# A planned attention-and-experts kernel: mask set-up split between engines, the last two query groups projected together, and a new order table

## The chip, the cores and the metric

One NeuronCore of a Trainium2 chip runs the whole program. The metric is the device time of one execution in microseconds (us), as the median of the runs. TensorE (PE) multiplies matrices; VectorE (DVE), ScalarE (ACT) and GpSimd (POOL) do the element-wise work; SyncE (SP) issues most DMA transfers.

## The reference

Two stages. The first is a linear recurrence over 768 positions for 4 batches and 8 heads of 48 channels; its output is laid out as x with 384 channels. The second runs four small experts on x, each a causal softmax attention of width 64 with its own output projection; a gate picks the top two of four and weighs them.

```
# recurrence, for each b, h
cur = outer(u*k_t, v_t);  y_t = r_t @ (state + cur)
state = w_t[:, None] * state + outer(k_t, v_t)
x = y as (B, S, H*D)
# experts
logits = x @ w_gate;  top 2 of 4;  w = softmax over the two
for e in range(4):
    q, k, v = x @ wq[e], x @ wk[e], x @ wv[e]
    a = softmax(causal(q @ k.T / 8))
    out += w[e] * ((a @ v) @ wo[e])     # where e is among the two
```

## The kernel before

**Tiling.** The recurrence runs in nine units (r0 to r8): batch 0 in pieces of 128, 256 and 384 positions, the other batches in two pieces of 384 each. Inside a unit positions go in chunks of 64: two scans along the positions (`suf`, L371, and `pre`, L375, on DVE) give the decay products, `kp` (L379 and L381) scales r and k by them, DMAs of `kp` onto itself rearrange it (L406), and TensorE computes the in-chunk scores (`aps`, L467, masked by `dec_mask` into `am`, L473), the state updates (`ups`, L495), and y as the carried part (`yy`, L538, from the faded states `ys`, L514) plus the in-chunk part (`yy`, L560). y is split into a high and a low part (`xh` L576, `xl` L578), because fp32 products are made here of three fast ones: high*high, low*high, high*low.

**The experts** run in ten groups (m0 to m9) of up to 384 positions. They follow the units, but the last unit is cut in two: m8 has 256 positions of batch 3, m9 the last 128. A group projects x to Q and K for two pairs of experts (`pp`, L658 and L661: 9 matmuls for each of 4 products, moving as many columns as the group has positions), to v and the gate's logits (`vp`, L688), then for each pair and each 128 positions makes scores (`sp`, L757), row maxima (L763, DVE), exponentials (`a`, L769, ACT), transposes (`tp`, L782, copied to `ATa`/`ATb` by L214 on ACT or L216 on DVE), and a*v (`yp`, L814). The gate's small operations stand at L712 to L731, the scaling by 1/sum at L832 to L835, its cut into three bf16 parts at L842 to L846; `gp` (L848) transposes it, `gT` (L850) copies that, `gb` (L860) spreads it with the 0/1 matrix `sel`. `yr` (L865 to L870) multiplies `yp` by it, `yh` (L874) and `yl` (L875) split it, `op` (L888) projects it, and `ob` (L214/L216) goes out by an SP DMA (L893).

**The order.** Nothing is ordered by a scheduler at run time. Each step is announced with `plan.add(kind, {engine: estimate}, function, reads, writes)`, and the table `ORDER` gives, for each place, the step (code // 5) and its engine (code % 5) among those that the step allows. Each engine works its own list in order. Tiles have names with a small number of buffers; a step that needs a buffer still in use waits. PE is kept busy before there is real work, and in gaps of the first units, by filler matmuls on a constant (`warm`): 14 of 512 columns (L931) and as many of 256 columns (L963) as a planned gap holds. These are fixed instructions in the program, 147 of the 256-column kind.

**Masks.** DVE makes all constants: `local` (L254 to L257) the identity and the mask of a chunk, `masks` (L274 to L280) in one block the bf16 identity, the causal mask `cmask`, `onehot`, its sum `pick`, `sel` and `tri`.

Of the kernel before, what the change touches and what calls it, by code (L numbers as in the profile page):

```python
# [10 lines left out]
F32 = mybir.dt.float32  # L11
# [8 lines left out]
C = 64  # L20
# [46 lines left out]
class Slot:  # L67
# [6 lines left out]
    def __call__(self):  # L74
# [17 lines left out]
BOTH = {"DVE": {"dg", "sm", "sa", "suf", "pre", "kt", "mr", "uk", "ur", "ux", "yl", "wsplitqk", "wsplitvg", "wsplito", "gate", "masks", "local"},  # L92
        "POOL": {"sm", "sa", "kt", "mr", "uk", "ur", "dg", "yl", "gate", "g4", "wsplitqk", "wsplitvg", "wsplito"}}
# [102 lines left out]
def rwkv_moe(ctx: ExitStack, tc: tile.TileContext, wkr, nat, uN, uT,  # L196
# [87 lines left out]
    def weights(n, src, cols, parts=1):  # L284
# [28 lines left out]
    def rwkv(k, v0, v1):  # L313
# [118 lines left out]
        def pairs(a, got):  # L432
# [42 lines left out]
            plan.add("am", {"DVE": 2 * t_dve(2 * nt * C)}, masked, aps + ["local"], [(am, b) for b in range(2)])  # L475
# [3 lines left out]
        def chain(nas):  # L479
# [26 lines left out]
            for c in range(nh):  # L506
# [18 lines left out]
        def outputs(got):  # L525
# [23 lines left out]
            for a in (1, 0):  # L549
# [21 lines left out]
                for q in range(2):  # L571
# [3 lines left out]
                    else:  # L575
                        plan.add("xh", {"ACT": t_act(2 * nt * C) + 42}, lambda e, q=q, view=view, summed=summed: nc.scalar.copy(view(0, q), summed(q)),  # L576
# [37 lines left out]
    def moe(k, v0, v1):  # L614
        b, s0, nt = GROUPS[k]
        W = nt * 128
        off = slice(s0 * 128, s0 * 128 + W)
# [12 lines left out]
        BT["s"] = BT["s"] + [s0]  # L630
# [4 lines left out]
        Q = [[sb([128, 384], F32R, f"Q{l}{ep}", f"Q{l}{n0}{ep}") for l in "hl"] for ep in range(2)]  # L635
# [12 lines left out]
        def proj(ep, qk):  # L648
            pp = mbank(f"pp{n0}{ep}{qk}")
            plan.sub = 2 * ep + qk  # L650
            cs = slice(ep * 128, (ep + 1) * 128)
            for k in (1, 0, 2):
                step(0.49 * nt / 3)

                def mm(e, k=k):
                    if plain:
                        w = wqf().rearrange("p (a k c) -> p a k c", a=2, k=3)
                        nc.tensor.matmul(pp()[:, 0:W], w[:, qk, k, cs], xx()[:, k, x0:x0 + W].bitcast(F32), start=k == 1, stop=k == 2)  # L658
# [16 lines left out]

        def vproj(i):
# [17 lines left out]
            plan.add("lg", {"DVE": 70}, lambda e: nc.vector.tensor_copy(lg()[:, i, :], vp()[:, 256:260]), [vp], [(lg, i)])  # L694

        def gates():
# [6 lines left out]

            V = nc.gpsimd
# [12 lines left out]
            def ranks(e):  # L717
                V.tensor_tensor(x_(ge), x_(lg), x_(m1)[:, :, None].to_broadcast([128, nt, E]), op=ALU.subtract)
# [4 lines left out]
            plan.add("gate", {"POOL": 1630}, ranks, lgk + ["masks", m1], [c1, c2, rank, ge])  # L723
# [4 lines left out]
            def norm(e):  # L728
# [464 lines left out]
```

## Time and profile before

| what | value |
|---|---|
| median of 3 runs | 328.79 us (328.03 to 329.52) |
| the profiled execution's own time | 327.85 us |
| its span | 326.1 us |
| PE busy | 316.8 us (97%) |
| DVE busy | 266.0 us (82%) |
| ACT busy | 197.9 us (61%) |
| POOL busy | 133.7 us (41%) |

The span runs from the first instruction to the last; 1.75 us of the execution's time lie around it. "Busy" counts the time in which an engine has an instruction under way; matmul ends are modelled, so a full PE is not PE at its peak. The chain of waits follows the work that ended last back to the start, and tells which engine or transfer each stretch waited for. Timeline rows give start and length in us; a bracket at the end gives how long the engine had been idle and which instruction ended that.

### The profile page before, as it was taken

The page shows a single profiled execution, that of the slowest core. Times are in us where ns is not written, and L with a number is a line of the kernel's source. Part 1 is how long each engine was busy: PE and PEld are TensorE (multiplying, and loading weights), DVE is VectorE, ACT ScalarE, POOL GpSimd, SP SyncE. Part 2 cuts the span into 40 slices and gives each one's busy share as a digit, 9 for nine tenths or more (in the row PEclk, how much of TensorE's full clock was granted, in tenths as well). Part 3 has the DMA queues.
Part 4 walks back from the last instruction along what each step waited for, and adds up shares of the span by engine and source line. Part 5 has one row for each costly group of instructions (what it writes and reads, how often), then busy time and mean ns, then how long its engine had stood idle before and what let it go on. Part 6 is the DMA issues. An engine that isn't in the chain of part 4 may idle for free.

```text
span 326.1 us, 12736 instructions
## 1 busy us (share of the span) xinstructions
PE 316.8 (97%) x5096; PEld 269.9 (83%) x5096; DVE 266.0 (82%) x803; ACT 197.9 (61%) x616; POOL 133.7 (41%) x312
## 2 busy tenths in 40 slices
PE   7999999999999999999999999999999999999985
PEld 3778879889896979879898778998898797987774
DVE  7899979987998799979899997867975774369831
ACT  2057474875898647973486766446646545378752
POOL 5543341565556252432655547434860001331420
PEclk9999999999999999999999999999999999999999
DMA  7954736156434643465655184223410300010021
GB/s 204 322 178 127 251 97 185 42 161 214 161 114 105 193 135 107 152 185 176 187 133 176 38 261 115 62 63 100 112 32 3 86 2 0 11 64 2 1 74 72
DMA packets 17866, 38.36 MB, mean 118 GB/s; under 512 B 3488, under 2 KB 8032, under 8 KB 17808
## 3 DMA queue, kind: packets, MB, share of 16 engines
q1 hardware_dynamic: 17424, 35.79, 36.8%
q0 software_dynamic: 384, 1.78, 1.6%
q8 instruction: 40, 0.66, 0.8%
q14 instruction: 18, 0.15, 0.2%
HBM read 28.14 MB, written 4.72 MB: 101 GB/s over the span
## 4 chain that ended last, share of the span: by engine, by line
PE 88%; DVE 5%; DMA 4%; issue 2%; ACT 0%; SPq 0%; POOL 0%; DVEq 0%; POOLq 0%; ACTq 0%
PE pp L661 16%; PE tp L782 12%; PE yp L814 12%; PE sp L757 11%; PE vp L688 8%; PE op L888 7%; PE yy L560 4%; PE aps L467 4%; PE yy L538 4%; PE ups L495 4%; PE ktp L397 2%; PE warm L963 2%; DMA kp<-kp 2%; DMA out_dram<-ob 1%; DVE a L763 1%
## 5 line engine op out<-in xcount | busy, mean ns | idle before, releaser
L769 ACT ACTIVATE a<-a,mx 128x128 f32<-128x128 f32 (+5 forms) x96 | 63.9, 668 | 23.8 <-DVE mx L763 23.3
L661 PE MATMUL pp<-xx,wh_qk 128*128 128x384 f32 (+2 forms) x216 | 60.6, 331 | 0.0
L782 PE MATMUL tp<-ident,a 128*128 128x128 f32 x336 | 50.0, 278 | 0.4 <-DVE mx L763 0.2
L763 DVE CUSTOM_DVE_ANT_0 a<-sp,cmask 128x384 f32<-128x384 f32 (+4 forms) x96 | 44.4, 495 | 6.7 <-PE sp L757 6.0
L782 PEld LDWEIGHTS tp<-ident,a 128*128 128x128 f32 x336 | 37.5, 141 | 6.3 <-ACT ATa L214 1.6
L661 PEld LDWEIGHTS pp<-xx,wh_qk 128*128 128x128 f32 x216 | 39.0, 189 | 1.1 <-issue 0.6
L814 PE MATMUL yp<-ATa,v_sb 128*64 128x384 f32 (+2 forms) x264 | 35.5, 406 | 0.0
L214 ACT COPY ATa<-tp 128x512 f32<-128x512 f32 (+3 forms) x64 | 29.2, 478 | 8.5 <-PE tp L782 7.6
L661 PE MATMUL pp<-xx,wl_qk 128*128 128x384 f32 (+2 forms) x108 | 34.3, 318 | 0.0
L688 PE MATMUL vp<-wh_vg,xx 128*128 128x260 f32 x138 | 30.8, 290 | 0.0
L814 PEld LDWEIGHTS yp<-ATa,v_sb 128*64 128x64 f32 x264 | 16.8, 136 | 14.1 <-issue 9.1
L371 DVE TENSOR_TENSOR_SCAN suf<-lt,one_suf 128x390 f32<-128x390 f32 (+2 forms) x27 | 24.9, 927 | 0.4 <-DMA lt<-in_wkr_dram 0.4
L375 DVE TENSOR_TENSOR_SCAN pre<-lt,inv_pre 128x390 f32<-128x390 f32 (+2 forms) x27 | 24.1, 893 | 0.3
L688 PEld LDWEIGHTS vp<-wh_vg,xx 128*128 128x128 f32 x138 | 23.5, 188 | 0.1
L757 PE MATMUL sp<-Kh,Qh 64*128 64x384 f32 (+4 forms) x128 | 23.5, 362 | 0.0
L216 DVE COPY ATa<-tp 128x512 f32<-128x512 f32 (+3 forms) x32 | 17.9, 570 | 5.2 <-PE tp L782 5.1
L875 POOL TENSOR_TENSOR yl<-yr,yh 128x384 fp32r<-128x384 f32 (+2 forms) x13 | 11.3, 882 | 25.8 <-ACT yh L874 18.8
L757 PE MATMUL sp<-Kh,Ql 64*128 64x384 f32 (+4 forms) x128 | 20.7, 319 | 0.0
L757 PE MATMUL sp<-Kl,Qh 64*128 64x384 f32 (+4 forms) x128 | 20.7, 319 | 0.0
L963 PE MATMUL warm<-one_suf 128*128 128x256 bf16 x147 | 19.2, 285 | 1.4 <-POOL one_suf L236 1.4
L661 PEld LDWEIGHTS pp<-xx,wl_qk 128*128 128x128 f32 x108 | 20.4, 189 | 0.0
L452 ACT ACTIVATE am<-ident,rk 128x64 f32<-128x64 f32 x76 | 19.8, 350 | 0.0
(387 smaller groups left out, 785.1 us busy)
## 6 DMA issues: line engine op xcount, KB each, us to landing
lt<-in_wkr_dram SPq DMA_DIRECT2D x21, 579.5 KB, 4.5
kr<-in_nat_dram SPq DMA_DIRECT2D x24, 288.0 KB, 3.4
out_dram<-ob SPq DMA_DIRECT2D x24, 192.0 KB, 2.1
nat<-in_nat_dram SPq DMA_DIRECT2D x14, 304.0 KB, 3.1
kp<-kp SPq DMA_DIRECT2D x42, 48.4 KB, 3.3
xx<-xx SPq DMA_DIRECT2D x42, 48.0 KB, 2.4
lt<-in_wkr_dram SPq DMA_DIRECT2D x3, 386.5 KB, 4.3
w_qk<-in_wqk_dram POOLq DMA_DIRECT2D x2, 384.0 KB, 5.9
```

What stands on the lines that cost most here:

```text
L214: nc.scalar.copy(o, i)
L371: plan.add("suf", {"DVE": t_scan(wb)}, lambda e: nc.vector.tensor_tensor_scan(rev(suf(), wb), rev(w_(), wb), rev(one_suf, wb), 0.0, op0=AL ...
L375: plan.add("pre", {"DVE": t_scan(wb)}, lambda e: nc.vector.tensor_tensor_scan(pre()[:, 0:kb], w_()[:, 0:kb], flat(inv_pre[:, 0:nh]), 0.0, ...
L661: nc.tensor.matmul(pp()[:, 0:W], w[:, qk, k, cs], xx()[:, k, x * xw + x0:x * xw + x0 + W], start=(k == 1 and j == 0), stop=(k == j == 2))
L688: nc.tensor.matmul(vp()[:, 0:260], xx()[:, k, x * xw + o.start:x * xw + o.stop], w[:, k, :], start=(k == 1 and j == 0), stop=(k == j == 2))
L757: nc.tensor.matmul(sps[x]()[:, 0:w], q()[p, t], k()[p, o], start=j == 0, stop=j == 2)
L763: plan.add("max", {"DVE": t_dve(w) + T_RED}, lambda e, x=x, a=a, mx=mx, h=h, o=o, m=m, sps=sps: nc.vector.tensor_tensor_reduce(a()[:, o], ...
L769: plan.add("exp", {"ACT": t_exp(n)}, lambda e, x=x, y=y, mx=mx, a=a: nc.scalar.activation(a()[:, 0:n], a()[:, 0:n], AF.Exp, bias=mx[-1](), ...
L782: nc.tensor.transpose(tp()[:, j * 128:(j + 1) * 128], a()[:, (j0 + j) * 128:(j0 + j + 1) * 128], ident)
L814: nc.tensor.matmul(yp()[e * 64:e * 64 + 64, lo:W], v_sb[ep]()[:, j, e * 64:e * 64 + 64], at, start=(j == 0), stop=(j == nj - 1))
L888: nc.tensor.matmul(op()[:, 0:DM], y()[:, t], w[:, ep, :], start=(j + ep == 0), stop=(j == 2 and ep == 1))
L963: nc.tensor.matmul(w()[:, 0:256], wz[:, 0:128], wz[:, 0:256], start=True, stop=True)
```

## The change

1. The set-up steps are cut apart. `local` becomes two steps and `masks` six, each with its own readers; `local`, `cmask`, `tri`, `onehot` and `pick` may run on DVE or POOL, `sel` and the bf16 identity on ACT or DVE. The reduction that made `pick` is two additions.
2. More steps may run on more engines: the high half of a weight (`wsplit`, ACT before) also on DVE and POOL; `ys` (L514) also on ACT, as four small multiplications; `xh`, the high halves of Q and K, `yr` also on DVE; `lg` and `gT` also on ACT; the gate's two small blocks and `g4` also on DVE; `yh` also on DVE and POOL.
3. Group m8 projects 384 columns, its own 256 and the 128 of m9; m9 projects no Q and K, and reads its columns of m8's tiles.
4. `ORDER` is new from its first entry.

```diff
-    def local(e):
-        for t, op in ((ident2, ALU.is_equal), (dec_mask, ALU.is_gt)):
-            nc.vector.tensor_scalar(t[0:64], d128[0:64, 0:C], 0.0, None, op0=op)
-            nc.vector.tensor_scalar(t[64:128], d128[64:128, 0:C], -64.0, None, op0=op)
+    def local(e, t, op):
+        E_[e].tensor_scalar(t[0:64], d128[0:64, 0:C], 0.0, None, op0=op)
+        E_[e].tensor_scalar(t[64:128], d128[64:128, 0:C], -64.0, None, op0=op)
...
-    def masks(e):
-        nc.vector.tensor_copy(identb, ident)
-        nc.vector.tensor_scalar(cmask[:, 384:512], d128, 0.0, -1.0e9, op0=ALU.is_gt, op1=ALU.mult)
-        nc.vector.tensor_scalar(onehot, dcol, drow, None, op0=ALU.is_equal)
-        nc.vector.tensor_reduce(pick, onehot.rearrange("p (a r) -> p r a", a=3), axis=AX.X, op=ALU.add)
-        nc.vector.tensor_copy(sel, pick[:, :, None].to_broadcast([128, 3 * E, HD]))
-        nc.vector.tensor_scalar(tri, tri, 0.0, None, op0=ALU.is_gt)
+    def picked(e):
+        E_[e].tensor_tensor(pick, onehot[:, 0:12], onehot[:, 12:24], op=ALU.add)
+        E_[e].tensor_tensor(pick, pick, onehot[:, 24:36], op=ALU.add)
...
+    masks = [(dict(POOL=350, DVE=200), lambda e: E_[e].tensor_scalar(cmask[:, 384:512], d128, 0.0, -1.0e9, op0=ALU.is_gt, op1=ALU.mult), [], "masks"),
...
+             (dict(ACT=700, DVE=500), lambda e: copy(e, sel, pick[:, :, None].to_broadcast([128, 3 * E, HD])), ["pick"], "sel"),
+             (dict(ACT=170, DVE=150), lambda e: copy(e, identb, ident), [], "identb")]
...
                 def faded(e, y=y, s=s, c=c):
+                    if e == "ACT":
+                        for p in range(NP):
+                            nc.scalar.mul(y[:, p * D:(p + 1) * D], s[0:112, p * D:(p + 1) * D], kp[0:112, p, K0 + c:K0 + c + 1])
+                        return
...
-        BT["s"] = BT["s"] + [s0]
+        tail = k == len(GROUPS) - 1
+        q0, PW = (W0, 0) if tail else (0, 384 if k == len(GROUPS) - 2 else W)
+        if not tail:
+            BT["s"] = BT["s"] + [s0]
...
-                        nc.tensor.matmul(pp()[:, 0:W], w[:, qk, k, cs], xx()[:, k, x * xw + x0:x * xw + x0 + W], start=(k == 1 and j == 0),
+                        nc.tensor.matmul(pp()[:, 0:PW], w[:, qk, k, cs], xx()[:, k, x * xw + x0:x * xw + x0 + PW], start=(k == 1 and j == 0),
...
-            plan.add("gate", {"POOL": 1630}, ranks, lgk + ["masks", m1], [c1, c2, rank, ge])
+            plan.add("gate", {"POOL": 1630, "DVE": 480}, ranks, lgk + ["tri", m1], [c1, c2, rank, ge])
...
-            t = slice(i * 128, (i + 1) * 128)
+            t = slice(q0 + i * 128, q0 + (i + 1) * 128)
...
-            plan.add("g4", {"POOL": 2450}, parts, [gg], [gg, g3])
+            plan.add("g4", {"POOL": 2450, "DVE": 480}, parts, [gg], [gg, g3])
...
-            plan.add("yh", {"ACT": t_act(W) + 42}, lambda e: nc.scalar.copy(h()[:, 0:W], yr()[:, 0:W]), [yr], [h])
+            plan.add("yh", {"ACT": t_act(W) + 42, "DVE": t_dve(W), "POOL": t_pool(W)}, lambda e: copy(e, h()[:, 0:W], yr()[:, 0:W]), [yr], [h])
...
-            for qk in range(2):
+            for qk in range(0 if tail else 2):
...
 ORDER = (
-    234, 448, 1, 159, 6, 154, 161, 175, 183, 202, 205, 166, 171, 17, 22, 27, 32, 37, 42, 47, 52, 57, 62, 67, 72, 77,
+    21, 8, 3, 564, 566, 588, 259, 266, 283, 189, 44, 339, 184, 191, 196, 205, 47, 52, 57, 62, 67, 72, 77, 82, 87, 92,
```

The new table gives the steps to the engines so: of the ten gate blocks of each kind six move from POOL to DVE, of the ten `g4` seven; 7 `xh`, 9 high halves of Q and K, 8 `yr` and 4 `yh` move from ACT to DVE, 8 `yh` from ACT to POOL; 14 `lg`, 4 `gT`, `sel` and the bf16 identity go from DVE to ACT, and 9 `ys` to ACT, 8 of them from DVE; 5 `kp`, 6 `kr` (L424 and L426, r and k scaled by u), 4 `us` (L519), the low half of one weight and both parts of `local` go from DVE to POOL. DVE has 860 instructions where it had 803. There are 149 fillers of 256 columns where there were 147, and 14 of 512 in both. The 36 projections of 256 columns and the 36 of 128 (m8 and m9) are 36 of 384.

**DVE at the start, before**: the block of masks (L256 to L280), then the first scans, those of r0's tiles `lt` (w, k and r of the unit; 130 columns are one of its parts).

```order
L257 TENSOR_SCALAR dec_mask<-d_73 64x64
L275 CAST identb<-ident 128x128
L276 TENSOR_SCALAR cmask<-d_73 128x128
L277 TENSOR_SCALAR onehot<-dcol,drow 128x36
L278 TENSOR_REDUCE pick<-onehot 128x12
L279 CAST sel<-pick 128x768
L280 TENSOR_SCALAR tri<-tri 128x16
L371 SCALAR_TENSOR_TENSOR suf_0_130<-lt_0_121,one_suf 128x130
L373 RECIPROCAL inv_pre<-suf_0_130 128x2
L375 SCALAR_TENSOR_TENSOR pre_0_152<-lt_0_121,inv_pre 128x130
L371 SCALAR_TENSOR_TENSOR suf_0_170<-lt_0_168,one_suf 128x260
```

DVE at the start, now (lines have moved by two: the scans are L373 and L377):

```order
L238 MEMSET inv_pre 128x390
L279 TENSOR_SCALAR onehot<-dcol,drow 128x36
L373 SCALAR_TENSOR_TENSOR suf_0_121<-lt_0_119,one_suf 128x260
L373 SCALAR_TENSOR_TENSOR suf_1_126<-lt_1_124,one_suf 128x130
L373 SCALAR_TENSOR_TENSOR suf_0_135<-lt_0_129,one_suf 128x130
L375 RECIPROCAL inv_pre<-suf_0_135 128x2
L381 TENSOR_TENSOR kp_96<-lt_1_124,suf_1_126 128x128
L377 SCALAR_TENSOR_TENSOR pre_0_153<-lt_0_129,inv_pre 128x130
L274 TENSOR_TENSOR pick<-onehot 128x12
```

One mask step is left ahead of the first scan, and that scan is now one of 260 columns, of unit r1. The constants stand between the scans or on POOL and ACT.

**SP at the start, before**, the loads of `lt` (131 and 256 columns are r0's, 773 r1's, 1159 r2's):

```order
L222 DMA lt_1_114<-in_wkr_dram 128x256
L222 DMA lt_0_121<-in_wkr_dram 128x256
L222 DMA lt_0_121<-in_wkr_dram 128x131
L222 DMA lt_0_168<-in_wkr_dram 128x773
L222 DMA lt_1_114<-in_wkr_dram 128x131
```

SP at the start, now:

```order
L222 DMA lt_0_119<-in_wkr_dram 128x773
L222 DMA lt_1_124<-in_wkr_dram 128x131
L222 DMA lt_0_129<-in_wkr_dram 128x256
L939 DMA u_81<-in_uT_dram 128x56
L222 DMA lt_2_132<-in_wkr_dram 128x256
L222 DMA lt_0_129<-in_wkr_dram 128x131
```

A load of r1 stands ahead of all of r0's.

**DVE at the end, before** (`gg` is the scaling of m9, `ob` an output tile of m7 and then of m8, `gT__6361` m9's gate):

```order
L835 TENSOR_TENSOR gg__6314<-gg__6314,ge__6069 128x4
L870 TENSOR_TENSOR yr_0_6324<-gb_0_6275,yr_0_6324 128x256
L870 TENSOR_TENSOR yr_1_6281<-gb_1_6296,yr_1_6281 128x256
L216 COPY ob_1_6348<-op_1_6307 128x384
L216 COPY ATa_10_6359<-tp_200_6299 128x4x128
L850 COPY gT__6361<-gp__6357 128x128
L216 COPY ob_1_6401<-op_1_6394 128x384
```

DVE at the end, now (the first row is m9's scaling, the five `g__6283` rows its cut into parts):

```order
L847 TENSOR_TENSOR gg__6279<-gg__6279,ge__6124 128x4
L854 MEMSET g__6283 128x64
L855 CAST g__6283<-gg__6279 128x4
L856 TENSOR_TENSOR gg__6279<-gg__6279,g__6283 128x4
L857 CAST g__6283<-gg__6279 128x4
L858 TENSOR_TENSOR g__6283<-gg__6279,g__6283 128x4
L216 COPY ob_0_6289<-op_0_6261 128x384
L887 TENSOR_TENSOR yl_0_6304<-yr_0_6147,yh_0_6302 128x256
L882 TENSOR_TENSOR yr_1_6270<-gb_1_6306,yr_1_6270 128x256
L216 COPY gT__6325<-gp__6323 128x128
```

The cut into parts, which POOL did, stands on DVE. One copy of `ob` stands between it and `gT`, as before, but of m7's first tile; the copies of m7's and m8's other tiles are on ACT.

## Rows read from the trace of the kernel before

**Rows 1.** The page: busy time by engine; the chain's shares by engine

```profile
PE 316.8 (97%) x5096; PEld 269.9 (83%) x5096; DVE 266.0 (82%) x803; ACT 197.9 (61%) x616; POOL 133.7 (41%) x312
...
PE 88%; DVE 5%; DMA 4%; issue 2%; ACT 0%; SPq 0%; POOL 0%; DVEq 0%; POOLq 0%; ACTq 0%
```

**Rows 2.** Windows: length; PE, PEld, DVE, ACT, POOL busy (instructions); clock; DMA

```profile
20.00:30.00 10.00, 9.17 (x173) 7.93 (x171) 10.00 (x20) 6.25 (x22) 4.38 (x7) 1.00 0.40 113
...
160.00:170.00 10.00, 10.00 (x386) 8.94 (x385) 9.62 (x30) 7.34 (x20) 5.00 (x9) 1.00 0.41 112
170.00:180.00 10.00, 10.00 (x78) 8.93 (x79) 10.00 (x31) 7.22 (x22) 5.90 (x11) 1.00 0.60 183
180.00:190.00 10.00, 10.00 (x243) 7.39 (x240) 9.90 (x28) 7.29 (x20) 5.64 (x17) 1.00 0.21 61
310.00:320.00 10.00, 8.83 (x80) 7.84 (x81) 3.15 (x11) 5.03 (x15) 2.19 (x6) 1.00 0.19 66
```

**Rows 3.** Chain of waits, projections of 384, 256 and 128 columns (start, us, matmuls)

```profile
109.04 2.12 PE pp L661 x12
...
260.91 1.75 PE pp L661 x15
...
291.55 0.95 PE pp L661 x9
```

**Rows 4.** Timeline of DVE, the first 6 us

```profile
1.63 0.19 DVE L256 TENSOR_SCALAR ident<-d 64x64 f32<-64x64 f32 x1 [0.36 <-POOL d L242]
...
3.60 0.58 DVE L279 CAST sel<-pick 128x768 bf16<-128x768 f32 x1
...
4.17 0.41 DVE L371 TENSOR_TENSOR_SCAN suf<-lt,one_suf 128x130 f32<-128x130 f32 x1
...
5.79 1.02 DVE L371 TENSOR_TENSOR_SCAN suf<-lt,one_suf 128x260 f32<-128x260 f32 x2 [0.38 <-DMA lt<-in_wkr_dram]
```

**Rows 5.** Chain of waits in the head (SPq: issuing of loads)

```profile
0.74 0.38 SPq L222
...
2.12 3.65 DMA lt<-in_wkr_dram
...
14.37 5.25 DMA kp<-kp
...
22.14 0.82 DVE ys L514
...
23.80 1.31 PE warm L963 x11
```

**Rows 6.** Timeline of PE in the head

```profile
23.01 0.45 PE L538 MATMUL yy<-kp,ys 48*64 48x64 f32 x16 [0.75 <-DVE ys L514]
...
25.19 0.68 PE L560 MATMUL yy<-am,nat 64*64 64x64 f32 x32
```

**Rows 7.** Timeline of DVE, 24 to 30 us: one form twice

```profile
24.94 1.87 DVE L295 TENSOR_TENSOR wl_qk<-w_qk,wh_qk 128x768 fp32r<-128x768 f32 x1
...
28.24 0.92 DVE L295 TENSOR_TENSOR wl_qk<-w_qk,wh_qk 128x768 fp32r<-128x768 f32 x1
```

**Rows 8.** Timeline of POOL beside it

```profile
24.98 1.00 POOL L384 TENSOR_TENSOR lt<-lt 128x384 f32<-128x384 f32 x1
```

**Rows 9.** Timeline of all engines in the tail

```profile
311.11 0.16 DVE L835 TENSOR_TENSOR gg__6314<-gg__6314,ge__6069 128x4 f32<-128x4 f32 x1
...
311.40 0.19 POOL L843 CAST g__6318<-gg__6314 128x4 bf16<-128x4 f32 x1 [2.76 <-DVE gg__6314 L835]
...
315.56 0.56 DVE L216 COPY ob<-op 128x384 f32<-128x384 f32 x1 [2.92 <-DMA out_dram<-ob]
...
316.89 0.22 PE L860 MATMUL gb<-gT__6361,sel 128*128 128x128 bf16 x1 [1.17 <-DVE gT__6361 L850]
```

**Rows 10.** Chain of waits in the tail: a store, and m8's `op`

```profile
311.60 3.83 DMA out_dram<-ob
...
317.34 2.10 PE op L888 x12
```

More of the change, by code (lines that the diff above doesn't have):

```diff
@@ L88 @@
          "SP": dict(PE=1600, DVE=1600, ACT=1600, POOL=1600, SP=1600)}
-BOTH = {"DVE": {"dg", "sm", "sa", "suf", "pre", "kt", "mr", "uk", "ur", "ux", "yl", "wsplitqk", "wsplitvg", "wsplito", "gate", "masks", "local"},
-        "POOL": {"sm", "sa", "kt", "mr", "uk", "ur", "dg", "yl", "gate", "g4", "wsplitqk", "wsplitvg", "wsplito"}}
+BOTH = {"DVE": {"dg", "yh", "g4", "sm", "sa", "suf", "pre", "kt", "mr", "uk", "ur", "ux", "yl", "wsplitqk", "wsplitvg", "wsplito", "gate", "masks", "local"},
+        "POOL": {"masks", "local", "sm", "sa", "kt", "mr", "uk", "ur", "dg", "yl", "gate", "g4", "wsplitqk", "wsplitvg", "wsplito"}}
 class Plan:
@@ L292, in weights @@
             load("wload" + n, lambda o=o: f()[:, o], src[:, o], cols // parts, [(f, c)])
-            plan.add("wsplit" + n, {"ACT": t_act(cols // parts) + 40}, lambda e, o=o: nc.scalar.copy(h[:, o], f()[:, o]),
+            plan.add("wsplit" + n, {"ACT": t_act(cols // parts) + 40, "DVE": t_dve(cols // parts), "POOL": t_pool(cols // parts)}, lambda e, o=o: copy(e, h[:, o], f()[:, o]),
                      [(f, c)], [("wh", n, c)])
@@ L474, in masked @@
                                               aps[h]()[:, 0:2 * nt * C].rearrange("p (a i j) -> p a i j", a=2, j=C))
-            plan.add("am", {"DVE": 2 * t_dve(2 * nt * C)}, masked, aps + ["local"], [(am, b) for b in range(2)])
+            plan.add("am", {"DVE": 2 * t_dve(2 * nt * C)}, masked, aps + ["dec"], [(am, b) for b in range(2)])
         car = [cars[(k + 1) % 2], cars[k % 2]]
@@ L575, in outputs @@
                     else:
-                        plan.add("xh", {"ACT": t_act(2 * nt * C) + 42}, lambda e, q=q, view=view, summed=summed: nc.scalar.copy(view(0, q), summed(q)),
+                        plan.add("xh", {"ACT": t_act(2 * nt * C) + 42, "DVE": t_dve(2 * nt * C)}, lambda e, q=q, view=view, summed=summed: copy(e, view(0, q), summed(q)),
                                  [yy[a][q]], [(xx, a, "h", q)])
@@ L616, in moe @@
         W = nt * 128
-        off = slice(s0 * 128, s0 * 128 + W)
+        W0 = GROUPS[-2][2] * 128
         xx, xk, x0, xw = XS[b, s0]
@@ L634, in rows @@
             return [y for y in xk if y[1] == (k if y[2] == "d" else k % 2)]
-        Q = [[sb([128, 384], F32R, f"Q{l}{ep}", f"Q{l}{n0}{ep}") for l in "hl"] for ep in range(2)]
+        if not tail:
+            BT["Q"] = [[sb([128, 384], F32R, f"Q{l}{ep}", f"Q{l}{n0}{ep}") for l in "hl"] for ep in range(2)]
+        Q = BT["Q"]
         lg = sb([128, 3, E], F32, "lg", f"lg{n0}")
@@ L693, in vproj @@
                          [vp], [(v_sb[ep], s0 + i)])
-            plan.add("lg", {"DVE": 70}, lambda e: nc.vector.tensor_copy(lg()[:, i, :], vp()[:, 256:260]), [vp], [(lg, i)])
+            plan.add("lg", {"DVE": 70, "ACT": 60}, lambda e: copy(e, lg()[:, i, :], vp()[:, 256:260]), [vp], [(lg, i)])
         def gates():
@@ L731, in norm @@
                 V.tensor_scalar(x_(gs), x_(gs), 1e-9, None, op0=ALU.add)
-            plan.add("gate", {"POOL": 875}, norm, [ge, c1], [gs, c1])
+            plan.add("gate", {"POOL": 875, "DVE": 270}, norm, [ge, c1], [gs, c1])
         def scores(ep, i):
-            t = slice(i * 128, (i + 1) * 128)
+            t = slice(q0 + i * 128, q0 + (i + 1) * 128)
             plan.sub = 3 * ep + i
@@ L922, in rwkv_moe @@
     plan.now = -1.0
-    plan.add("local", {"DVE": 1060}, local, [], ["local"])
-    plan.add("masks", {"DVE": 1400}, masks, [], ["masks"])
+    plan.add("local", {"DVE": 530, "POOL": 650}, lambda e: local(e, ident2, ALU.is_equal), [], ["local"])
+    plan.add("local", {"DVE": 530, "POOL": 650}, lambda e: local(e, dec_mask, ALU.is_gt), [], ["dec"])
+    for engs, fn, reads, name in masks:
+        plan.add("masks", engs, fn, reads, [name])
     plan.add("ldu2", {"SP": 475, "ACT": 475}, lambda e: E_[e].dma_start(u2, uT.rearrange("p (j c) -> p j c", j=7)), [], ["u2"], xfer=190.0)
```

37 lines of the change are left out of this document (21 added, 16 removed), and 220 rows, old and new, of the table ORDER.

## Prediction

> **What bounds the kernel now.** I read the busy shares first, then the chain of waits, then windows. TensorE (PE) is busy 97% of the span and carries 88% of the chain; VectorE (DVE) carries 5%, transfers 4%, and the other engines round to nothing [rows 1]. So the time is PE's work plus the places where PE has none. The windows say where these are: PE is full in the middle (10.00 of 10 us in the three windows from 160 us on); it has gaps in the head (9.17 between 20 and 30 us) and in the tail (8.83 between 310 and 320 us) [rows 2]. Three things can therefore shorten the kernel: fewer or cheaper matmuls, an earlier start of the first real work (the fillers hide that the head is a wait: PE counts as busy while it multiplies constants), and a tail with fewer waits. A change of engine for an element-wise step in the middle can win almost nothing, since PE does not wait there; it can only lose, if it makes DVE late. DVE is itself at 9.62, 10.00 and 9.90 of 10 us between 160 and 190 us, and full from 20 to 30 us [rows 2].
>
> **Joint projection, about -1.7 us.** Before, m8 has 36 matmuls of 256 columns and m9 36 of 128; now there are 36 of 384. The pace is read from the chain, which gives stretches of them back to back: 12 of 384 columns take 2.12 us, 177 ns each; 15 of 256 take 1.75 us, 117 ns; 9 of 128 take 0.95 us, 106 ns [rows 3]. The small form is far dearer than its columns: it hardly beats the one of twice the size. The sum: 36 x 117 = 4.21 and 36 x 106 = 3.82, together 8.03; 36 x 177 = 6.37; difference 1.66. All are on PE, and PE is full or nearly so in this stretch, so the whole of it shows. What could take some back: m9's projections were filler between attention steps of m7 and m8, and the exponentials of these may now be waited for; and the joint ones must come before m8's scores. Bounds: 1.3 to 2.1. The evacuations also fall from two per product to one, off PE's path.
>
> **Mask set-up, at most half a microsecond by itself.** The obvious reading is that DVE spends 2.5 us on masks (from 1.63 us to 4.17 us [rows 4]) and that the scans start that much sooner. That is not what the rows say. The next scan in the row, at 5.79 us, waited 0.38 us for a landing, with all masks done [rows 4]; the loads set the pace until then. The scan at 4.17 us started right behind the last mask, so it could have been somewhat sooner, but its data cannot have come much before: the first load was issued by about 1.1 us, and a load of r1, issued at 2.12 us, took 3.65 us to land [rows 5]. I give the masks' removal 0 to 0.5 us. Against it stands the new order of loads: a 386 KB load of r1 is issued ahead of r0's small ones, and the first scan on DVE is r1's. If that scan holds DVE until r1's data land, r0's scans start later than now by up to about 0.6 us (first issued, by 1.12 us, and 3.65 us under way [rows 5], it lands at 4.8 us; r0's scan began at 4.17).
>
> **The rest of the head, -1.5 us with the masks in it.** From the first scan to 14 us DVE is the chain, then the `kp` transfer of 5.25 us, then DVE again, at 22.14 us with `ys` [rows 5]. PE waited 0.75 us for that `ys`, ran y's first half at 23.01 us, 11 fillers, and the second half at 25.19 us [rows 6]. From 20 to 30 us DVE never rests [rows 2], so each microsecond taken from DVE before `ys` brings y, and all behind it, forward by as much. The change takes `sel` (0.58 us [rows 4]), the other constants, and some `ys` and low halves off DVE there, about 2 us of work; `ys` runs partly on ACT, which has room (6.25 of 10 us busy [rows 2]). The ends: +0.5 us if the late load of r0 outweighs it, -2.5 us if all of the relief shows and the 5.25 us transfer also starts sooner. I take -1.5, nearer to the gain, since DVE is the releaser in the row and the masks stand early in its list. The fillers are fixed instructions: 149 instead of 147 at 1.31 / 11 = 0.12 us each [rows 5] cost +0.2 us, and where they stand behind data that come early they go on running.
>
> **Body, 0 with a width of 1.5.** DVE takes over six gate chains, seven `g4` chains, 7 `xh`, 9 halves of Q and K, 8 `yr`, 4 `yh` and gives away less; by the durations of the nearest forms in the trace (0.16 us for a small operation, up to 0.56 us for a copy of 384 columns, both [rows 9]) I estimate some 8 us more for DVE over the whole program, of 60 us that it has free (326.1 - 266.0 [rows 1]). ACT loses some 2 us, POOL is about as before. Work in the free part is hidden; PE's wait would show it where it is not. To win, there is only PE's idle time outside head and tail, about nothing in the windows shown. So the middle is 0, and the ends are -1.5 and +1.5 us.
>
> What the trace says of moving steps to POOL: the same subtraction took 1.87 us on DVE while a POOL instruction of 1.00 us ran, and 0.92 us alone [rows 7, 8]. The difference, 0.95 us, is nearly the POOL instruction's length. The Trainium skill has a rule for this (SBUF — State Buffer, "SBUF: two separate sides"): DVE with two inputs in SBUF and a POOL operation that reads SBUF take an exclusive lock on a shared pair of ports, and the loser waits for the whole instruction. The rows agree. By that rule the 5 `kp`, 6 `kr`, 4 `us` and 8 `yh` given to POOL, 23 steps, would each cost DVE up to a POOL instruction's length again, some 1 us by the row, 23 us in all; it speaks against these moves, and it would change the sum only by the part of them that falls where DVE is full.
>
> **Tail, -0.9 us.** Now, m9's gate is late for a reason that has nothing to do with gates: DVE's copy of `ob` stands ahead of `gT__6361`, and waits 2.92 us for a store (3.83 us in the chain [rows 10]) that still reads the buffer; so `gT` is late, and PE stands 1.17 us before `gb` [rows 9]. In the new order m7's copies are mostly on ACT and the tile ahead of `gT` is its first, so this wait should go. Three things are late next. DVE now cuts m9's scaling itself: 11 small operations at 0.16 to 0.2 us, 2 us, where before three on DVE (from 311.11 us) and five on POOL (the first at 311.40 us, 0.19 us each [rows 9]) took about as long. ACT's copies of `ob` still wait for earlier stores, and behind one of them stands an `ATa` copy that m9's `yp` needs: up to 2.92 us there, of which m8's 12 `op` matmuls on PE hide 2.10 [rows 10]. And the last `yr`, `yh`, `yl` all stand on DVE, which saves the hops to ACT, a few tenths. Following the new rows by hand with these durations I get an end about 1 us sooner, and take -0.9; ends -1.2 (the whole wait of 1.17) and +0.5 us (ACT's wait takes its place and more).
>
> **Sum.** -1.7 - 1.5 + 0.2 + 0 - 0.9 = -3.9 us. Against the profiled execution, 327.85 us, that is 323.95; the median is 328.79, 0.94 above it, and I carry the same difference: 324.9 us.
>
> **Rivals.**
> The head gives nothing (**326.4**, chance 0.20): the first r0 scans wait for loads behind r1's, and fillers stand where data come sooner. Then only -1.7 + 0.2 - 0.9 = -2.4 remains. For it: the wait for a landing at 5.79 us [rows 4] and the fillers that stand in the chain [rows 5]. Against it: DVE's 100% from 20 us on.
> Only the projections, **about 328** (0.15): head as in the rival above, the tail's wait changes its place, fillers +0.2 and a few waits behind projections eat the rest of 1.7. This is within 0.5%, which is about what a measurement of this kernel can tell from no change.
> DVE becomes the bound (**331**, 0.08), the slower side: between 160 and 190 us DVE has 0.48 us free of 30 [rows 2]. If the work it takes over, or meetings with POOL at 0.95 us each, falls there and in the two or three stretches like it, PE waits for row maxima. It decides against the change when such waits exceed the 3.9 us of gains; with 6.1 us of them, six or seven meetings, the time is 328.79 - 3.9 + 6.1 = 331.0. Against it: there are 60 us free elsewhere, and gates and `g4`, whose small POOL operations met DVE's, leave POOL.
> The new order also removes waits that the modelled ends of matmuls hide (**321.5**, 0.15): head at its end of -2.5, body at -1.5, tail at -1.2, joint projections at -2.1, fillers +0.2 give -7.1, that is 321.7, and I set 321.5.
>
> **How the numbers follow.** The forecast itself has 0.42; with 0.20, 0.15, 0.08 and 0.15 that is 1. Faster by over 0.5% means below 327.15: the forecast (0.42), the better order (0.15), most of the head rival (0.15), a little of the projections rival (0.02), 0.74. Slower by over 0.5% means above 330.4: DVE as the bound, 0.07 of its 0.08. The rest, 0.19, is no change. For the range I leave out the slower case, half of the projections rival's upper side and the lower part of the better order, together under 0.2: 320.8 to 328.6.
>
> **What will show it.** Joint projections right: 36 matmuls of 384 columns for m8, none for m9, PE's busy time lower by about 1.7 us, no new idle time of PE beside them. Head right: y's second half (25.19 us now) begins between 22.7 and 25 us, with DVE's `ys` earlier; wrong if it begins at 25.2 us or later, or if the first scans of DVE wait past 5 us. Tail right: no DVE wait of more than a microsecond for a store, and `gb` of m9 without PE idle before it. Body right: PE at 9.9 of 10 us or more in every window from 40 to 300 us; wrong if PE waits there for DVE's maxima or for ACT. The whole is wrong if PE's busy time rises elsewhere, or if DVE near 190 us lags with PE waiting.

## The result: 331.59 us after 329.03, slower by 0.5%

The changed kernel takes 331.59 us (median of 20 runs, 327.79 to 333.45), the kernel before 329.03 us beside it (20 runs, 326.73 to 330.93). The ratio is 1.0052, 95% interval 1.0026 to 1.0077. The forecast was 324.9 us, with a range up to 328.6. The profiled execution took 331.89 us; its span is 330.0 us, 3.9 more than before. Medians are of all runs; the ratios leave out those over 1.5% above the least time of their kernel, so the 0.5% stands for 1.7 us where the medians lie 2.56 us apart.

One remark is needed for every number below: the granted clock of TensorE differs from run to run. The new kernel's five runs at a mean clock of 0.997 or more took 328.0 us, its twelve at 0.990 or less 332.2 us. Of the 136 runs of the kernel before that stand beside the experiments, the 64 at 0.997 or more took 328.2 us, and only six were at 0.990 or less. So at the whole clock the two kernels take the same time, and the new one loses in the runs in which its clock fell.

The page of the new kernel: busy time, the chain's shares, and PE's granted clock in 40 slices (against [rows 1]).

```profile
PE 317.1 (96%) x5062; PEld 269.7 (82%) x5062; DVE 276.4 (84%) x860; ACT 197.9 (60%) x628; POOL 134.8 (41%) x259
...
PE 80%; DVE 9%; issue 3%; ACT 3%; POOL 2%; DMA 1%; SPq 1%; DVEq 0%; POOLq 0%
...
PEclk9999599999999999999999999999999999999999
```

PE's share of the chain fell from 88% to 80%; DVE, ACT and POOL took it. PE's busy time did not fall, although 1.7 us of projections are gone, and one slice runs at half the clock. The windows, with the columns of [rows 2], say where:

```profile
0.00:10.00 10.00, 8.55 (x42) 4.81 (x42) 5.24 (x19) 1.68 (x3) 5.73 (x25) 1.00 0.75 221
...
30.00:40.00 10.00, 8.63 (x129) 8.01 (x130) 5.96 (x13) 4.79 (x19) 4.00 (x5) 0.70 0.37 106
140.00:150.00 10.00, 7.82 (x199) 5.95 (x190) 6.42 (x16) 6.44 (x25) 5.69 (x9) 1.00 0.54 155
...
310.00:320.00 10.00, 10.00 (x96) 8.37 (x95) 8.45 (x35) 4.90 (x13) 0.40 (x1) 1.00 0.01 2
```

DVE is less busy in the first ten microseconds (5.24, before 8.07); PE has gaps and a mean clock of 0.70 from 30 to 40 us, and waits 2.18 us from 140 to 150 us. The tail is full, where [rows 2] had 8.83. The head, in PE's timeline of the new kernel:

```profile
20.35 0.33 PE L497 MATMUL ups<-nat,kts 64*64 64x48 f32 x8 [1.33 <-DVE kts L216]
...
25.27 0.68 PE L566 MATMUL yy<-am,nat 64*64 64x64 f32 x32
...
26.72 3.01 PE L977 MATMUL warm<-one_suf 128*128 128x256 bf16 x26
31.37 0.52 PE L399 MATMUL ktp<-ident,kp 128*128 128x128 f32 x3 [1.64 <-ACT am L454]
```

The second half of r0's y starts where it did (25.27 us against 25.19 [rows 6]). Then 26 fillers run out, and PE stands 1.64 us for r2's first keys (`ktp`). In the kernel before these start 4.2 us sooner:

```profile
27.16 0.53 PE L397 MATMUL ktp<-ident,kp 128*128 128x128 f32 x3
```

From 34 to 41 us the new kernel's clock is at 0.50, one level down (1.2 GHz for 2.4); one window of it (length, PE busy, granted clock, DMA share, GB/s):

```profile
36.00:38.00 2.00, 2.00 (x9) 0.50 0.31 115
```

Around 140 us the new kernel's ACT and PE read:

```profile
141.95 1.54 ACT L454 ACTIVATE am<-ident,rk 128x64 f32<-128x64 f32 x6 [2.88 <-PE yy L566]
...
143.39 0.60 ACT L781 ACTIVATE a<-a,mx 128x384 f32<-128x384 f32 x1
...
144.63 0.44 PE L794 MATMUL tp<-ident,a 128*128 128x128 f32 x2 [2.06 <-ACT a L781]
```

ACT's list has r5's `am` block ahead of two of m3's exponentials. The block needs a buffer that r4's `yy` on PE must free; so ACT idles 2.88 us with the exponentials' data at hand, and PE then waits 2.06 us for them.

### The profile page after: what moved, and what is told of

Its sections match the earlier page's. It is cut to its first block, busy times and chain, and to the rows that moved or that the text cites. A ratio compares the mean times of both kernels' runs of the same rounds, so it can differ in the third digit from the quotient of the medians.

```text
span 330.0 us, 12661 instructions
## 1 busy us (share of the span) xinstructions
PE 317.1 (96%) x5062; PEld 269.7 (82%) x5062; DVE 276.4 (84%) x860; ACT 197.9 (60%) x628; POOL 134.8 (41%) x259
## 4 chain that ended last, share of the span: by engine, by line
PE 80%; DVE 9%; issue 3%; ACT 3%; POOL 2%; DMA 1%; SPq 1%; DVEq 0%; POOLq 0%
PE pp L673 13%; PE tp L794 11%; PE yp L826 11%; PE sp L769 10%; PE op L900 7%; PE vp L700 7%; PE ups L497 4%; PE aps L469 4%; PE yy L544 3%; PE yy L566 3%; PE ktp L399 2%; DVE suf L373 2%; DVE pre L377 2%; ACT am L454 1%; PE rp L392 1%
## 5 line engine op out<-in xcount | busy, mean ns | idle before, releaser
L673 PE MATMUL pp<-xx,wh_qk 128*128 128x384 f32 (+1 forms) x192 | 56.2, 343 | 0.0
L214 ACT COPY ATa<-tp 128x512 f32<-128x512 f32 (+3 forms) x68 | 31.0, 487 | 13.3 <-PE tp L794 12.8
L673 PEld LDWEIGHTS pp<-xx,wh_qk 128*128 128x128 f32 x192 | 34.9, 189 | 0.1
L673 PE MATMUL pp<-xx,wl_qk 128*128 128x384 f32 (+1 forms) x96 | 31.6, 329 | 0.0
L377 DVE TENSOR_TENSOR_SCAN pre<-lt,inv_pre 128x390 f32<-128x390 f32 (+2 forms) x27 | 25.9, 960 | 0.1
L373 DVE TENSOR_TENSOR_SCAN suf<-lt,one_suf 128x390 f32<-128x390 f32 (+2 forms) x27 | 24.1, 902 | 1.4 <-DMA lt<-in_wkr_dram 1.4
L454 ACT ACTIVATE am<-ident,rk 128x64 f32<-128x64 f32 x72 | 18.4, 341 | 7.5 <-PE yy L566 2.9
L216 DVE COPY ATa<-tp 128x512 f32<-128x512 f32 (+3 forms) x28 | 15.1, 544 | 8.8 <-PE tp L794 8.8
L525 POOL TENSOR_TENSOR us<-us,ys 112x192 f32<-112x192 f32 x21 | 12.6, 600 | 19.8 <-DVE pre L377 7.6
L700 PE MATMUL vp<-wl_vg,xx 128*128 128x260 f32 x69 | 19.5, 283 | 0.0
L584 DVE TENSOR_TENSOR xx<-yy,xx 112x384 fp32r<-112x384 f32 (+1 forms) x32 | 16.1, 532 | 4.0 <-ACT xx L214 3.9
```

The costliest lines, as they stand in the source:

```text
L214: nc.scalar.copy(o, i)
L373: plan.add("suf", {"DVE": t_scan(wb)}, lambda e: nc.vector.tensor_tensor_scan(rev(suf(), wb), rev(w_(), wb), rev(one_suf, wb), 0.0, op0=AL ...
L377: plan.add("pre", {"DVE": t_scan(wb)}, lambda e: nc.vector.tensor_tensor_scan(pre()[:, 0:kb], w_()[:, 0:kb], flat(inv_pre[:, 0:nh]), 0.0, ...
L454: nc.scalar.mul(am()[:, h, b, i], ident2, v[:, i, h:h + 1])
L673: nc.tensor.matmul(pp()[:, 0:PW], w[:, qk, k, cs], xx()[:, k, x * xw + x0:x * xw + x0 + PW], start=(k == 1 and j == 0), stop=(k == j == 2))
L700: nc.tensor.matmul(vp()[:, 0:260], xx()[:, k, x * xw + o.start:x * xw + o.stop], w[:, k, :], start=(k == 1 and j == 0), stop=(k == j == 2))
```

## The experiments

Two theories were set against each other. Head: the new order loses in the first 55 us, and the clock with it. Body: it loses by waits of ACT and DVE in the middle. Medians are of 6 to 12 runs; ratios, with 95% intervals, are to the kernel before on the same chip. Where two kernels are compared, the difference of their ratios is taken, times 329 us.

**e1, joint projection alone.**

```diff
 kernel before
+m8 projects 384 columns, m9 none
```

> The kernel before with one change: m8 projects 384 columns and m9 none; the masks on DVE, the engines and the order of all other steps are those of before (the sum of the one-hot rows is two additions). Both theories, head (A: the new order loses in the first 60 us, by late loads of r0, and PE's wait at 30 us is followed by half the clock) and body (B: it loses by waits for ACT and DVE in the middle), expect the forecast of this term: -1.7 us (-1.3 to -2.1), ratio 0.995. If the ratio is 1.000, the term itself was wrong.

Measured: 327.09 us, before 328.87; 0.9946 (0.9909 to 0.9982). The term is right: -1.8 us (by the interval, -3.0 to -0.6).

**e2, head of before.**

```diff
 new kernel
-first 55 us in the new order
+first 55 us in the order and on the engines of before
```

> The new kernel, but every step that the order of before has in its first 55 us stands as it did there, on its engine of before; the rest is in the new order, with the joint projection. A (head): the loss goes, the granted clock stays at 1.00 from 30 to 60 us, and the time is about 326 us, ratio 0.992, 5 us below the new kernel. B (body): the time stays at 329 to 331 us, ratio 1.000 to 1.005.

Measured: 328.26 us, 0.998 (0.9954 to 1.0007); the runs lie between 327.6 and 328.7. The head holds 2.4 us of the new kernel's time. What is left, 1.1 us above e1, is the new order behind 55 us; the intervals of e2 and e1 overlap, and e6 below bears it out. So both theories have a part. The clock did not stay up, as theory A had it: in e2's profiled execution it is at 0.62 and 0.52 from 28 to 32 us, and it falls again right behind PE's wait for ACT, which e2 shares with the new kernel (2.06 us, until 139.76 us); the window has the columns of the one above:

```profile
142.00:146.00 4.00, 4.00 (x64) 0.68 0.45 114
```

**e3, start of before.**

```diff
 new kernel
-first 10 us in the new order
+first 10 us as before (r0's loads first, masks as one block)
```

> The new kernel, but only the first 10 us stand as before: r0's loads first, the masks as one block on DVE; from there on the new order (11 fillers fewer come out of the plan). If the late loads of r0 carry the head's loss: DVE is busy 8 of the first 10 us as before, r2's first keys on PE start 3 us sooner (28 us), the clock stays up, and the time is about 327 us. If the rest of the head's order carries it: r2's keys stay at 30 us or later, 330 us or more.

Measured: 333.04 us, 1.0109 (1.0051 to 1.0167), six runs, five of them at a clock of 0.989 or less. r0's first product on DVE starts at 6.61 us instead of 7.40, and yet r2's keys start at 32.78 us. Undoing the start does not cure the head. But e3 has 11 fillers fewer, which can cost time by itself (e11), so what the late loads alone cost is not shown here.

**e4 and e5, fillers where PE stood idle.**

```diff
 new kernel
+16 fillers ahead of r2's first keys          (e4 and e5)
+14 fillers ahead of r0's state updates       (e5)
```

> The new kernel with 16 more fillers of 256 columns ahead of r2's first keys, where PE stood idle 1.64 us before 31.37 us. If the idle time is what the clock fell for: granted clock 1.00 between 34 and 41 us, time 328.2 us in all runs (the new kernel's runs at clock 1.00 are 327.8 to 328.4). If the clock falls for the few columns of the matmuls after it: clock 0.50 again, 331.6 us.

> The new kernel with 30 more fillers: 14 ahead of r0's state updates, in which PE stood idle 1.33 us before 20.35 us, and 16 ahead of r2's first keys (1.64 us before 31.37 us). With the second place alone the clock was whole in only a few runs (329.8 us). If idle time of PE in the head is what the clock falls for: most runs at granted clock 0.997 or more and the median at 328.0 to 328.6 us. If it falls for other reasons: a spread from 327.4 to 335 us and a median near 330 us, as before.

Measured: e4 329.75 us (1.0007, 0.9966 to 1.0047), in single runs from 327.4 to 335.4; its profiled execution has the clock at half from 22 to 25 us instead, behind the other gap. e5 329.78 us (1.002, 0.9989 to 1.0052), with no run below 0.993 and all between 328.6 and 331.4. So with both gaps filled the deep falls are gone, as the theory of idle time says; but only four of the twelve runs are at 0.997 or more, not most, and the median did not reach 328.0 to 328.6.

**e6 and e9, one step moved on ACT,** in e2 and in the new kernel.

```diff
 ACT, around 142 us
-L454 ACTIVATE am_0_2894<-ident_84,rk_0_2414 128x64 x6
 L781 ACTIVATE a_32_2761,asum__2499<-a_32_2761,mx_320_2762 128x384
 L781 ACTIVATE a_21_2764,asum__2499<-a_21_2764,mx_210_2765 128x256
 L214 COPY yr_0<-yp_0
+L454 ACTIVATE am_0_2894<-ident_84,rk_0_2414 128x64 x6
```

> The kernel e2 (head of before, rest new) with one step moved: on ACT, r5's `am` block (six small steps of 0.25 us, which waits for r4's last use of the buffer on PE) stands behind m3's two exponentials and `yr` instead of ahead of them. PE waited 2.1 us there (136 to 140 us in e2) for the exponentials. If that wait is on the path: 1.5 to 2.1 us less than e2, 326.2 to 326.8 us. If the wait only moves to the next step: 328.2 us as e2.

> The new kernel with the one step of e6 moved (r5's `am` block on ACT behind m3's exponentials), the rest as it is. If the wait there costs the new kernel as it cost e2 (1.8 us): 329.8 us against 331.6. If the clock in the head hides it or the runs spread too far: 331 us.

Measured: e6 326.46 us (0.9922, 0.9891 to 0.9953), 1.9 less than e2, with intervals that do not overlap. e9 328.83 us (1.0006, 0.9975 to 1.0037), 1.5 less than the new kernel (2.8 by the medians of all runs). One step of 1.5 us, three places too early in a list, cost about as much as the joint projection had gained.

**e7, gates back on POOL** (in e2).

```diff
-DVE: 16 gate blocks and cuts into parts, m1 to m9
+POOL: the same, at the same places
```

> The kernel e2 with the gates' small blocks and the cut into parts back on POOL wherever the new order gave them to DVE from m1 on (16 steps; 8 fillers fewer). If DVE's added work and its meetings with POOL make the middle's waits: DVE's busy time falls by 5 to 8 us and the time by 1 to 1.5 us, to about 327 us. If DVE's work there is hidden: 328.2 us or, since POOL takes longer for them, up to 1 us more.

Measured: 329.73 us, 1.003 (1.0001 to 1.0059), 1.6 more than e2. The page of e7, and the longest of PE's waits in it (total us, times, longest):

```profile
PE 314.8 (96%) x5058; PEld 268.7 (82%) x5058; DVE 269.8 (82%) x791; ACT 193.9 (59%) x621; POOL 144.8 (44%) x322
...
PE yy L566 <- POOL nat L553: 2.2, 2, 2.0
```

DVE did get some 8 us less to do (277.7 in e2), and it helped nothing visible. But e7 made a loss of its own: at 190.84 us PE waits 2.00 us for a small POOL step (`nat`) that stands behind a gate's cut into parts, which itself waited for DVE. In e2 this wait is 0.2 us. So e7 does not show that giving DVE the gates was a gain; it shows once more what one step costs that waits ahead of a ready one.

**e8, the new tail alone.**

```diff
 e1
-from 250 us on the order of before
+from 250 us on the new order
```

> The kernel before with the joint projection up to 250 us, and the new order from there. Forecast for the tail: 0.9 us less than e1 (327.1 us), so 326.2 us; the trace of the new kernel gives 1.4 us less idle time of PE between 300 and 320 us, so 325.7 us. If the new tail's waits take the place of the old ones: 327.1 us.

Measured: 329.88 us (1.0023, 0.9989 to 1.0057), 2.5 more than e1. The seam itself made a wait:

```profile
264.77 0.77 PE L794 MATMUL tp<-ident,a 128*128 128x128 f32 x5 [2.61 <-ACT a L781]
```

Without these 2.61 us the time would be about that of e1, if the whole of them is on the path. So the tail gave about nothing, as far as a kernel with a seam can say.

**e10, masks alone,** and **e12, loads alone** (each in e1).

```diff
+e10: masks spread over POOL, ACT and DVE's later list
+e12: SP: r1's 386 KB load ahead of r0's, the first eight loads as in the new kernel
```

> The kernel e1 (before with the joint projection) and the masks of the new kernel: identity and chunk mask on POOL, `sel` and the bf16 identity on ACT, the others between r0's scans on DVE (4 more fillers come out of the plan). By the rows of before (the first scans wait for loads): 0 to -0.5 us against e1, 326.6 to 327.1 us. If the obvious reading held (2.5 us off DVE at the start): 325 us. If it changes nothing but the fillers: 327.5 us.

> The kernel e1 with only the first eight loads on SP in the new order, r1's 386 KB load ahead of r0's (11 more fillers come out of the plan); masks and scans as before. By the prediction: the head starts up to 0.6 us later, 327.1 to 327.7 us. By the new kernel's trace, where r0's first products waited for a landing until 7.4 us: 2 to 3 us later, 329 to 330 us, if r0's scans set the head. 327.1 us if they do not.

Measured: e10 325.94 us (0.9924, 0.9896 to 0.9952, six runs), 0.7 less than e1, with intervals that overlap widely: a gain is not shown. DVE in e10:

```profile
3.60 0.43 DVE L373 TENSOR_TENSOR_SCAN suf<-lt,one_suf 128x130 f32<-128x130 f32 x1 [0.27 <-DMA lt<-in_wkr_dram]
...
6.15 1.02 DVE L373 TENSOR_TENSOR_SCAN suf<-lt,one_suf 128x260 f32<-128x260 f32 x2 [1.11 <-DMA lt<-in_wkr_dram]
```

The first scan is 0.57 us earlier than in [rows 4] and waits for its load, the next one waits 1.11 us instead of 0.38: the loads do set the pace. r0's y is not earlier either (24.72 us, in e1 24.42). e12: 329.16 us (0.9976, 0.9946 to 1.0006), 1.0 above e1 by the ratios and 2.1 by the medians, its runs from 325.5 to 334.5; these intervals overlap too, but r0's y starts 1.1 us later than in e1 (25.52 us). Its first scan reads:

```profile
5.78 0.43 DVE L373 TENSOR_TENSOR_SCAN suf<-lt,one_suf 128x130 f32<-128x130 f32 x1 [1.23 <-DMA lt<-in_wkr_dram]
```

1.6 us later than in [rows 4], where the prediction allowed 0.6.

**e11, the clock's price on the kernel before.**

```diff
 kernel before
-24 fillers ahead of r0's y
```

> The kernel before without the 24 fillers ahead of r0's y (19.1 to 21.8 us in its trace): PE then stands idle about 3.5 us there, with no other change of order. If idle time of PE in the head lowers the clock later and that costs time: granted clock at 0.50 for some us within the next 15 us and a median of 331 to 333 us. If the fillers are worth nothing: 329 us.

Measured: 333.91 us (1.0108, 1.0069 to 1.0146), all seven runs at 0.988 or less; by the ratio that is 3.6 us, by the medians 5.0. PE's windows in its profiled execution (length, busy, granted clock, DMA share, GB/s):

```profile
20.00:30.00 10.00, 8.19 (x101) 0.57 0.38 89
30.00:40.00 10.00, 10.00 (x131) 0.57 0.35 126
```

PE stood 0.55, 0.91 and 1.79 us where the fillers had been, and its clock was at half for most of the next 17 us. Not one real instruction differs: idle time of PE in the head costs 3.6 us or more, by the clock.

**e13 and e14, loads of before in the new kernel,** e14 with the step on ACT moved too.

```diff
 new kernel
+SP: r0's loads first, as before; DVE: r1's first scan behind r0's
+ACT: r5's am block as in e6                 (e14 only)
```

> The new kernel with the first loads on SP in the order of before (r0's ahead), and r1's first scan behind r0's scans on DVE; everything else as in the new kernel (13 more fillers come out of the plan). If the load order carries the head's loss (e12: 2.1 us on the kernel with joint projection): the time falls by 2 to 3.5 us, to 328.1 to 329.6 us, and deep clock falls get rare. If the rest of the head's order carries it (e3 went to 333): 331 us or more.

> e13 and the step moved on ACT as in e6 and e9. If the two causes add: 1.8 to 2.8 us less than e13, 326 to 327.5 us, and then these two account for the whole loss against the forecast's 324.9 but for the tail. If the head is not cured by the loads: 328.8 us as e9.

Measured: e13 331.30 us (1.0059, 1.0019 to 1.0098), e14 327.82 us (1.0003, 0.9974 to 1.0032). e13 did not free the start: DVE's list begins with another piece of r0 than before, and its first scan waits 2.41 us for that piece, until 5.74 us. The first product starts at 6.68 us instead of 7.40, r0's y is later (26.03 us, behind more fillers), and PE still waits 1.65 us for r2's keys. So no gain came of the loads in this order, and a clean test of them is missing. The step on ACT is worth 1.8 us here (3.5 by the medians).

**e16 and e17, DVE's subtractions behind r2's keys,** e17 with the step on ACT moved too.

```diff
 DVE, around 26 to 30 us
-L297 TENSOR_TENSOR wl_qk<-w_qk,wh_qk 128x768
 L377 SCALAR_TENSOR_TENSOR pre_2<-lt_2_357,inv_pre 128x390
-L297 TENSOR_TENSOR wl_qk<-w_qk,wh_qk 128x768
 L381 TENSOR_TENSOR kp_96<-lt_0_246,suf_0_257 128x384
+L297 TENSOR_TENSOR wl_qk<-w_qk,wh_qk 128x768 x2
```

> The new kernel with one change in the head: on DVE the two subtractions of w_qk's low half (1.15 and 0.93 us) stand behind r2's first keys (`kp`) instead of ahead of them. PE waited 1.64 us for these keys before 31.37 us. If DVE is what r2's keys wait for: that wait is 0 to 0.4 us, clock falls get rarer, and the time is 328 to 330 us against 331.6. If the wait is ACT's (`am`, the releaser that the row names): nothing changes, 331.6 us.

> The new kernel with both moved: DVE's two subtractions as in e16 and ACT's `am` block as in e9 (328.8 us alone). If the two waits of PE (1.64 and 2.06 us) and the clock that falls with them are the loss: 326.5 to 327.5 us, ratio 0.993 to 0.995. If the head has more to it: 328 us or more.

Measured: e16 330.42 us (1.0058, 1.0021 to 1.0095), by its ratio no better than the new kernel, by the medians 1.2 us; e17 327.26 us (0.9962, 0.9934 to 0.999). In e16 r2's keys read:

```profile
29.11 0.52 PE L399 MATMUL ktp<-ident,kp 128*128 128x128 f32 x3 [0.44 <-DVE kp L381]
```

The wait shrank from 1.64 to 0.44 us by moving DVE alone, and the keys start 2.26 us sooner, with 14 fillers fewer ahead of them: ACT, which the row of the new kernel names, was not what PE waited for. The `kp` itself, begun just ahead of POOL's next product (28.60 us):

```profile
28.44 0.53 DVE L381 TENSOR_TENSOR kp<-lt,suf 128x384 f32<-128x384 f32 x1
```

It ends 0.14 us before PE starts, as in the new kernel. With both steps moved, 3.0 us of the new kernel's time are gone, 1.4 more than with the step on ACT alone (e9, with overlapping intervals); three list entries turn it from slower than before into faster.

**e15, the parts that won.**

```diff
 e10 up to 55 us (head of before, masks spread, joint projection)
+from there the new order, r5's am block as in e6
```

> A kernel from the parts that won alone: head of before with the masks of the new kernel between the scans (e10), joint projection, the new order from 55 us on with the step moved on ACT (e6). If the parts add: 326.5 - 1.1 = 325.3 us, below both kernels and all experiments. If the gain of the masks was a gain of the clock in that run of kernels alone: 326.5 us.

Measured: 325.55 us, 0.9919 (0.9888 to 0.995), 4.4 us below the new kernel and 2.7 below the one before. By the ratio that is e6 (0.9922): the masks, which e15 has besides, add nothing that shows. PE's waits over a microsecond, from the view of what it waited for (total us, times, longest), are one, the start's; the three longest:

```profile
PE warm L977 <- POOL one_suf L236: 1.4, 1, 1.4
PE ktp L399 <- POOL kp L381: 0.9, 1, 0.9
PE ktp L399 <- DVE Kl L685: 0.5, 1, 0.5
```

## Why the prediction was wrong, step by step

In the prediction's terms, and by the ratios of the experiments: joint projection -1.8 us (e1); the new order behind 55 us +1.1 (e2 less e1), in it the one ACT step +1.5 to +1.9; the head +2.4 (the new kernel less e2). The sum is +1.7, the 0.5% measured; it must come out so, since each difference starts where the last ended, and is no test.

**Joint projection: right.** -1.7 forecast, -1.8 measured. The pace of 384 columns is the one of [rows 3], now for m8 in the new kernel's chain:

```profile
268.35 2.09 PE pp L673 x12
```

**Rest of the head, -1.5 forecast, +2.4 measured: the step that failed.** "Each microsecond taken from DVE before `ys` brings y, and all behind it, forward" counted what was taken off DVE and not what the new list puts ahead of the steps that PE waits for. y's second half came at 25.27 us for 25.19, the prediction's own sign of being wrong, and r2's keys behind it at 31.37 us for 27.16. The start and the neighbourhood of r2's keys, on DVE and POOL of the new kernel:

```profile
5.73 0.51 DVE L373 TENSOR_TENSOR_SCAN suf<-lt,one_suf 128x130 f32<-128x130 f32 x1 [0.82 <-DMA lt<-in_wkr_dram]
...
7.40 0.29 DVE L381 TENSOR_TENSOR kp<-lt,suf 128x128 f32<-128x128 f32 x1 [0.89 <-DMA lt<-in_wkr_dram]
...
29.03 0.93 DVE L297 TENSOR_TENSOR wl_qk<-w_qk,wh_qk 128x768 fp32r<-128x768 f32 x1
29.88 1.35 DVE L381 TENSOR_TENSOR kp<-lt,suf 128x384 f32<-128x384 f32 x1
```

```profile
29.19 1.62 POOL L386 TENSOR_TENSOR lt<-lt 128x384 f32<-128x384 f32 x1
```

r0's second scan waits for its data until 5.73 us and its first product until 7.40 us (6.93 before), so the relief by the masks is spent before it counts. Later two subtractions for weights that can wait stand ahead of r2's `kp`, and that `kp`, 0.53 us in e16, takes 1.35 us beside a POOL product. That is the lock of the Trainium skill (SBUF — State Buffer, "SBUF: two separate sides"), and the row agrees: `kp` ends 0.42 us after the POOL product.

How the 2.4 us divide is open in part. Moving the subtractions gained 1.4 us with the ACT step moved (e17 less e9) and nothing clear without (e16); e16 still has PE wait 1.3 us for `kts` and 1.1 us for `xx`, which no run took away.

**The clock: the term that was missing.** The sum had no price for PE standing idle in the head, though the kernel before spends 161 fillers there. The granted clock was 1.00 in every window of [rows 2], and the prediction read it as given. The new kernel's runs at 0.997 or more take 328.0 us, within the range and as e2; those at 0.990 or less 4.2 us more. So the later keys cost little by themselves, and most of the head's loss is the clock that falls behind PE's waits.

**Body, 0 +- 1.5: +1.1, in its range by luck.** The forecast looked at DVE, whose busy time rose by 10.4 us where 8 were estimated, from 160 to 190 us, where PE has now no gap either (10.00 in each window). What cost was a step of ACT behind a wait, at 142 us; no term of the sum went through ACT's list for steps that wait for a buffer. The rival "DVE becomes the bound" has the right sign and the wrong engine: PE is full in the very windows that it named.

**Tail, -0.9 forecast, about 0 measured (e8).** The step that failed is the price of [rows 9]: DVE's 2.92 us wait hung on a store of 3.83 us [rows 10]. The view of the tile `ob` from 300 us on gives issue to landing; first the kernel before, then e1, which has the tail of before:

```profile
DMA to landing us min/median/max: 1.8/1.9/3.8
```

```profile
DMA to landing us min/median/max: 1.8/1.9/2.0
```

And the same copy in e1's timeline:

```profile
315.55 0.56 DVE L216 COPY ob<-op 128x384 f32<-128x384 f32 x1 [0.93 <-DMA out_dram<-ob]
```

With an ordinary store DVE waits 0.93 us, and PE does not wait at all. The 1.17 us that the forecast wanted to win were one execution's late store. Late stores do recur: e7, e10, e11 and e12 have one of 2.9 to 3.4 us in their tails, but PE waits behind none of them. PE has no wait in e1's tail either, and not by the new order.

**Masks, 0 to -0.5:** the mechanism as forecast, the time 0.7 us better (e10) or 0.1 (e15 beside e6), neither clear of noise. **Loads, up to +0.6:** mis-sized; the pieces of r0 that its second scan and its first product wait for came sixth and seventh in the row of issues, and e12 shows +1.0 us, with y 1.1 us later. **Fillers:** two more, as forecast.

## What to carry to other kernels

When a list is reordered, follow each engine's new list for steps that wait with ready work behind them; one such step cost 1.5 to 1.9 us here (3.2 between e16 and e17), as much as the real saving of 1.8. Before crediting a wait on a transfer, compare its landing with the median of its kind: one execution's late store is no gain to be had. Where PE is kept busy by fillers, idle time of PE has a second price in the clock, and a forecast needs a term for it.

## What the runs showed of the hardware

The price of an idle TensorE: taking 24 fillers out of the kernel before cost 3.6 us by the ratio and 5.0 by the medians (e11), with the clock at half from 22 to 38 us. But idle time alone does not decide: e13 and e14 have the same instructions up to about 130 us and the same wait of 1.65 us for r2's keys, and yet in e13's profiled execution the clock is at 0.50 from 35 to 41 us, and in e14's it is whole. Nor did it fall behind the new kernel's 2.06 us wait for ACT, as it did behind the same wait in e2. What else decides is open. Seven of twelve runs of e13 have a mean clock below 0.991, and one of twelve of e14; that need not come from the head, since e14 lacks the wait for ACT.

A row's releaser can mislead: PE's 1.64 us were put down to ACT's `am`, but moving DVE's steps alone took 1.20 us of them away and brought the keys 2.26 us forward (e16).
